# Five token chunks of a fused attention and feed-forward kernel, cut at other rows, with longer attention units

## The chip, the cores and the metric

The kernel runs on one core of a Trainium2 chip. The metric is the device time of one execution in microseconds (us). TensorE does the matmuls; VectorE, ScalarE and GpSimd (POOL) do element work; SyncE (SP) issues nearly all transfers.

## The reference

Four batches of eight heads, 576 positions, head dimension 64. Heads 0 to 3 attend to the last 32 positions (local), heads 4 to 7 to the positions of the same remainder by 32 (strided). The result, 2304 tokens by 512, goes through two feed-forwards:

```python
scores = np.where(masks[None, :, :, :], scale * np.matmul(q, k.transpose(0, 1, 3, 2)), -1000000000.0)
attn = np.exp(scores - np.max(scores, axis=-1, keepdims=True))
x = attn / (np.sum(attn, axis=-1, keepdims=True) + 1e-09) @ v
...
g = x @ w_gate
x = (g * (1.0 / (1.0 + np.exp(-g))) * (x @ w_val) @ w_out)
...
h = np.maximum(np.maximum(x @ w1, x @ w2), x @ w3)
out = h @ w_out
```

Sizes: w_gate and w_val 512 x 1536, w_out 1536 x 512; in the second, w1, w2, w3 512 x 768 and w_out 768 x 512.

## The kernel before

Work is counted in rows of 32 tokens: 72 rows, in the order ORDER. `ROWS` cuts that order into five chunks; `width(c)` is 32 times the rows of chunk c, at most 512 tokens.

**First feed-forward.** Its three weights lie in 12 blocks of 128 hidden units, counted by f. Every operand is split into a high and a low fp32r part, and a product is three matmuls (L701 high by high, L702, L703). For a chunk c and an f, `emit_gate` does 12 matmuls over the width of the chunk into a bank `ps_g`, and ScalarE's silu (L720) makes `ht`; `emit_val` does 12 into `ps_v`, and VectorE's L727 multiplies `ht` by it; ScalarE copies the high part (L733), GpSimd subtracts for the low part (L737); `emit_out` does 12 matmuls into four banks `ps_y`, one f later. That makes 36 matmuls for an f and 432 for a chunk. Gate and val banks come in turn from a pool of two, so val(f+1) reuses the bank that L727(f) reads.

**The x tiles.** `x_tile(c)` gives the high and low x of a chunk, with the tag `c % 2`: chunk c and chunk c+2 share memory. So writes into chunk 3's x wait until the last matmul that reads chunk 1's.

**Attention.** Chunk 0 and 1's attention comes ahead, in an order written out by hand. For c = 2 to 4, `attention_steps(c)` gives 15 lists of steps, and list i is emitted with slot (c-1) x 12 + i - 3, that is, during the chunk before. Local heads go in blocks of one or two groups of two rows: scores on TensorE (L393), minima against the mask on VectorE (L429), exponentials on ScalarE (L440), L445, L446 and L450 normalise on VectorE, then a transpose (L462), its copy (L467), the product with v (L504), and the copies into x, high by ScalarE (L516) and low by VectorE (L522). All of it goes through `att`, a pool of two banks. `scores_with` and `outputs_with` take two blocks at once; they call `claimed`, which asks for both banks and touches each by a tiny ScalarE copy (L309).

Strided rows that TensorE does not do go as `Unit`s of up to six rows on VectorE: products with the keys (L600) and their reductions (L603), one softmax for the unit (L608 to L615, with the exponential L610 on ScalarE), products with the values (L622) and reductions (L625), then transposes by threes (L632) into an `att` bank, and copies into x (L643 high, L644 low). The first matmuls of a gate read x's two blocks of local heads, the others the strided heads' blocks.

**Second weights.** `later` holds 60 steps that turn the second feed-forward's weights into the seven pieces of its scheme; each group of five steps is two loads, two conversions and a combination, then the parts (L281, L282) with their stores to `wsdr`. `PACE[c]` says how many steps are due in each f of chunk c (f below 10).

**The end.** From f = 10 of chunk 4 on the order is written by hand; in the slot before, the remaining w_v and w_o are reloaded, `load_y` (L838) loads the first tiles of y and `load_w` (L851) the second weights. The second feed-forward's matmuls are 128x384 (L858). Between, the scheduler places each engine's instructions.

Of the kernel before, what the change touches and what calls it, by code (L numbers as in the profile page):

```python
# [7 lines left out]
F32 = mybir.dt.float32  # L8
# [8 lines left out]
B, H, S, D = 4, 8, 576, 64  # L17
# [3 lines left out]
NI = S // STRIDE  # L21

LR = 2
# [8 lines left out]

PASSES = [1, 2, 0]

PACE = [0, 0.7, 1.4, 1.4, 3.1]

PACED = 10
NK = DM // 128

ROWS = [0, 16, 30, 44, 58, 72]  # L40


ORDER = [*range(16), *range(18, 72), 16, 17]
AT = {row: n for n, row in enumerate(ORDER)}
NC = len(ROWS) - 1
N = STRIDE * max(ROWS[c + 1] - ROWS[c] for c in range(NC))

ON_PE = [(0, 16, 4), (1, 14, 4)]

EARLY = -(-ROWS[1] // LR)  # L50

DEEP = [*range(NK // 2, NK), *range(NK // 2)]

# [40 lines left out]
def tile_attention_swiglu_maxout(  # L94
# [38 lines left out]
    tiny = sub(attn, "tiny", 2, side="right")  # L133
# [33 lines left out]

    ydr = [dram.tile([128, NK, width(c)], F32, name=f"ydr{c}") for c in range(NC)]

# [11 lines left out]
    st_p, pr_p = [], []  # L181
# [116 lines left out]
    def x_tile(c):  # L298
        if c not in xt:
            xt[c] = tuple(x_p.tile([128, NK, N], F32R, name=f"x{p}", tag=f"x{p}{c % 2}") for p in "hl")  # L300
        return xt[c]
# [222 lines left out]
    def local_block(g, home=None):  # L524


        def dst(src, us):
            for c, i0, i1, o in pieces(LR * g[0], LR * (g[-1] + 1)):
                t, w = slice(i0 * STRIDE, i1 * STRIDE), slice(o * STRIDE, (o + i1 - i0) * STRIDE)
                xh, xl = x_tile(c)  # L530
                yield xh[:, 0:2, t], xl[:, 0:2, t], src[:, :, w]

        return Block((locqk, locv), g[0], KB, [mask[0 if n % (NI // LR) == 0 else 1] for n in g], dst, home=home)
# [24 lines left out]
    def joined(ns):  # L558
        out = []
        for n in ns:  # L560
            if out and len(out[-1]) < 2 and out[-1][-1] + 1 == n:
                out[-1].append(n)
            else:
                out.append([n])
        return out

    class Unit:
# [36 lines left out]

        def softmax(self):
            sc, n, jn = self.sc, self.n, self.jn
            mx = tiny.tile([128, 6], F32, name="smx")[:, :n]
            nc.vector.tensor_reduce(mx, sc, AX.X, ALU.max)  # L608
            nc.vector.tensor_tensor(sc, sc, mx[:, :, None].to_broadcast([128, n, jn]), ALU.subtract)
            nc.scalar.activation(sc, sc, AF.Exp, scale=SCALE)  # L610
            sums = tiny.tile([128, 6], F32, name="ssum")[:, :n]
            nc.vector.tensor_reduce(sums, sc, AX.X, ALU.add)
            nc.vector.tensor_scalar(sums, sums, 1.0e-9, None, ALU.add)
            nc.vector.reciprocal(sums, sums)
            nc.vector.tensor_tensor(sc, sc, sums[:, :, None].to_broadcast([128, n, jn]), ALU.mult)  # L615
            self.o = st_p[0].tile([128, 6, D], F32, name="sto")

        def pv(self, r, eng):
            i = self.i0 + r
# [25 lines left out]

    def attention_blocks(c):
        rows = ORDER[ROWS[c]:ROWS[c + 1]]
        blocks = [local_block(g) for g in joined([r // LR for r in rows[::LR]])]
        if c == 1:
            blocks += [strided_block((st1qk, st1v), 1, g) for g in pairs(range(STRIDE // ON_PE[1][2]))]  # L650
        return blocks

    def attention_steps(c):

        steps = [[] for _ in range(15)]
        rows = ORDER[ROWS[c]:ROWS[c + 1]]
        eng = nc.vector
        blocks = attention_blocks(c)
        at = [0, 0, 4, 4, 8]
        for n, blk in enumerate(blocks):  # L660
            s0 = at[n]
            wait = 3 if c == 2 and s0 == 0 else 0
            steps[max(0, s0 - 2)].append(blk.load)
            if n % 2 and s0 == at[n - 1]:
                steps[s0].append(lambda a=blocks[n - 1], b=blk: a.scores_with(b))
                steps[s0 + wait].append(lambda a=blocks[n - 1], b=blk: (a.softmax(eng), b.softmax(eng)))
            elif n + 1 == len(blocks) or s0 != at[n + 1]:
                steps[s0].append(lambda blk=blk: (blk.scores(), blk.softmax(eng)))
            steps[s0 + (4 if wait else 1)].append(lambda blk=blk: blk.transpose(nc.scalar))
            if n % 2 and s0 == at[n - 1]:  # L670
                steps[s0 + (5 if wait else 2)].append(lambda a=blocks[n - 1], b=blk: (a.outputs_with(b), a.split(), b.split()))
            elif n + 1 == len(blocks) or s0 != at[n + 1]:
                steps[s0 + 2].append(blk.pv)
        units = []
        on_pe = {n: rows for n, rows, _ in ON_PE}
        left = [r for r in rows if r % NI >= on_pe.get(r // NI, 0)]
        while left:
            i = left[0]
            n = 1
            while n < len(left) and left[n] == i + n and (i + n) % NI % 6:  # L680
                n += 1
            units.append(Unit(i // NI, i % NI, n))
            left = left[n:]
        s0 = 0
        for u in units:
            steps[s0].append(u.load)
            steps[s0].append(u.begin)
            for r in range(u.n):
                steps[s0 + (2 * r // u.n)].append(lambda u=u, r=r: u.qk(r, eng))
            steps[s0 + 2].append(u.softmax)  # L690
            for r in range(u.n):
                steps[s0 + 2 + (2 * r // u.n)].append(lambda u=u, r=r: u.pv(r, eng))
            for r in range(0, u.n, 3):
                steps[s0 + 5 + r // 3].append(lambda u=u, r=r: u.out(r))
            s0 += 4
        return steps


# [5 lines left out]

    def linear(ps, w, x, n, ks=range(NK)):
        xh, xl = x
# [60 lines left out]
    def emit_out(c, f):  # L767
# [3 lines left out]
        if f == 0:  # L771
            yacc[c] = [acc.tile([128, 512], F32, name="ps_y", tag="acc") for _ in range(NK)]
        for m in range(NK):
            ms = slice(m * 128, (m + 1) * 128)
# [246 lines left out]
    if True:  # L1021
        blocks = [strided_block((st0,), 0, g, True) for g in pairs(range(STRIDE // ON_PE[0][2]))]
# [3 lines left out]
        def evictor(i):  # L1026
            return nc.vector if i in (0, 2, 3, 5, 6, 7) else nc.scalar

        steps = {
            "k": lambda i: nc.sync.dma_start(cst[:, halves[i]], shape_consts[:, halves[i]]),  # L1030
            "l": lambda i: blocks[i].load_qk(),
            "m": lambda i: blocks[i].load_v(),
            "S": lambda i: blocks[i].scores(),
            "W": lambda i: blocks[i].scores_beside(blocks[i + 1]),
            "M": lambda i: blocks[i].least(),
            "E": lambda i: blocks[i].exps(),
            "R": lambda i: blocks[i].inverse(),
# [42 lines left out]
        for s, (c, f) in enumerate(slots):  # L1080
# [7 lines left out]
            with ExitStack() as tied:  # L1088
                if c == 0:
                    tied.enter_context(tc.issue_after(last_val[0]))  # L1090
                for step in fill.get(s, []):
                    step()
            if c > 0 and f < PACED:
                due += PACE[c]
                with ExitStack() as tied:
# [25 lines left out]
    if True:  # L1121
# [13 lines left out]
        before = None  # L1135
        for p in range(NP):
            h2.clear()
            for g in range(NFP):
                for i in range(3):
# [12 lines left out]
                    before = grp  # L1152
            y = outputs(p, grp, y)
            before = None
# [99 lines left out]
```

## Time and profile before

| what | value |
| --- | --- |
| median of 3 runs | 785.83 us |
| lowest and highest | 784.95 and 786.53 us |
| the profiled execution | 786.19 us |
| its span, first to last instruction | 784.4 us |
| TensorE busy | 767.7 us |
| VectorE busy | 613.2 us |
| ScalarE busy | 400.9 us |
| GpSimd busy | 230.8 us |

The profile is of one execution. Starts count from the span's beginning. In it chunk 1's first gate begins at 140.54 us, chunk 2's at 237.47, chunk 3's at 334.42, chunk 4's at 428.47; the second feed-forward's steady part follows from 519.62 us. A matmul's duration in the profile overlaps the next one's, so its pace is read from start to start.

### The profile page before, as it was taken

To read this page: it belongs to the slowest core of one execution; us is meant where nothing else is said; L and a number is where in the kernel's file an instruction comes from. 1 tells how busy PE (TensorE), PEld (TensorE's weight loads), DVE (VectorE), ACT (ScalarE), POOL (GpSimd) and SP (SyncE) were. 2 spreads that over 40 slices of the span, in tenths; PEclk is the share of its full clock that TensorE was granted. 3 is DMA by queue.
4 is the path that set the end of the run, shared out by engine and by line. 5 is a ranking of instruction groups with operands and counts; after the bars stand their busy time and mean duration, and the time that the engine had idled before them with its cause. 6 is when DMAs were issued, how large, how long until landed. Compare 5 with 4: busy or idle time off the path is not lost.

```text
span 784.4 us, 13322 instructions
## 1 busy us (share of the span) xinstructions
PE 767.7 (98%) x4642; PEld 705.2 (90%) x4642; DVE 613.2 (78%) x1206; ACT 400.9 (51%) x925; POOL 230.8 (29%) x226
## 2 busy tenths in 40 slices
PE   5899999999999999999999999999999999999998
PEld 4677788888998998988899999999999999999998
DVE  5999999798959899799796777754689377855683
ACT  6999997644544636545342545432335233433342
POOL 2533332012221432325242556420124111321120
PEclk9999999999999999999999999999999999999999
DMA  9989886987657896847787999997675976878722
GB/s 274 369 277 320 306 351 236 372 252 230 221 188 222 285 293 222 267 168 256 255 286 267 314 378 392 342 377 274 242 276 199 414 270 264 276 280 355 276 101 81
DMA packets 75595, 216.26 MB, mean 276 GB/s; under 512 B 8488, under 2 KB 42024, under 8 KB 70920
## 3 DMA queue, kind: packets, MB, share of 16 engines
q1 hardware_dynamic: 75528, 215.41, 77.8%
q8 instruction: 37, 0.61, 0.3%
q14 instruction: 30, 0.25, 0.1%
HBM read 171.34 MB, written 44.04 MB: 275 GB/s over the span
## 4 chain that ended last, share of the span: by engine, by line
PE 85%; DVE 9%; ACT 3%; issue 1%; DMA 1%; POOL 1%; SPq 0%; DVEq 0%; ACTq 0%
PE ps_a L858 19%; PE ps_c L858 10%; PE ps_v L701 6%; PE ps_y L701 5%; PE ps_y L702 5%; PE ps_v L703 5%; PE ps_y L703 5%; PE ps_v L702 5%; PE ps_g L703 5%; PE ps_g L702 5%; PE ps_g L701 5%; PE ps_b L858 5%; DVE w L231 1%; PE ps_a L504 1%; PE ps_a L462 1%
## 5 line engine op out<-in xcount | busy, mean ns | idle before, releaser
L737 POOL TENSOR_TENSOR hl<-ht,hh 128x448 fp32r<-128x448 f32 x47 | 62.0, 1320 | 215.3 <-ACT hh L733 197.2
L869 ACT ACTIVATE s<-ps_a 128x384 f32<-128x384 f32 x99 | 48.5, 490 | 131.7 <-PE ps_a L858 131.7
L701 PE MATMUL ps_v<-xh,w_v 128*128 128x448 f32 (+1 forms) x240 | 90.8, 379 | 2.1 <-DVE ht L727 1.8
L701 PE MATMUL ps_g<-xh,wh_g 128*128 128x448 f32 (+1 forms) x240 | 89.9, 375 | 1.2 <-DVE ht L760 1.1
L702 PE MATMUL ps_y<-hl,w_o 128*128 128x448 f32 (+1 forms) x240 | 89.6, 373 | 0.0
L702 PE MATMUL ps_g<-xl,wh_g 128*128 128x448 f32 (+1 forms) x240 | 89.5, 373 | 0.0
L703 PE MATMUL ps_g<-xh,wl_g 128*128 128x448 f32 (+1 forms) x240 | 89.3, 372 | 0.0
L703 PE MATMUL ps_v<-xh,w_v 128*128 128x448 f32 (+1 forms) x240 | 89.2, 372 | 0.1
L703 PE MATMUL ps_y<-hh,w_o 128*128 128x448 f32 (+1 forms) x240 | 89.2, 372 | 0.0
L702 PE MATMUL ps_v<-xl,w_v 128*128 128x448 f32 (+1 forms) x240 | 88.9, 370 | 0.0
L733 ACT ACTIVATE hh<-ht 128x448 fp32r<-128x448 f32 (+1 forms) x60 | 35.3, 588 | 94.8 <-DVE ht L727 85.4
L701 PE MATMUL ps_y<-hh,w_o 128*128 128x448 f32 (+1 forms) x240 | 83.6, 376 | 0.0
L808 POOL TENSOR_TENSOR rT<-t,rT 128x384 f32<-128x384 f32 x9 | 12.5, 1392 | 147.1 <-DVE rT L807 147.1
L858 PE MATMUL ps_a<-y0hT,wr 128*128 128x384 f32 x162 | 54.1, 334 | 0.0
L858 PE MATMUL ps_a<-y1hT,wr 128*128 128x384 f32 x162 | 54.1, 334 | 0.0
L701 PEld LDWEIGHTS ps_v<-xh,w_v 128*128 128x128 f32 x240 | 45.1, 188 | 8.1 <-DVE ht L727 2.4
L701 PEld LDWEIGHTS ps_g<-xh,wh_g 128*128 128x128 f32 x240 | 45.1, 188 | 6.8 <-DVE ht L760 1.5
L703 PEld LDWEIGHTS ps_v<-xh,w_v 128*128 128x128 f32 x240 | 45.1, 188 | 5.5 <-DVE w_v L251 0.5
L701 PEld LDWEIGHTS ps_y<-hh,w_o 128*128 128x128 f32 x240 | 45.1, 188 | 5.2
L702 PEld LDWEIGHTS ps_g<-xl,wh_g 128*128 128x128 f32 x240 | 45.1, 188 | 5.1 <-DVE xl L522 0.3
L703 PEld LDWEIGHTS ps_g<-xh,wl_g 128*128 128x128 f32 x240 | 45.1, 188 | 5.1
L703 PEld LDWEIGHTS ps_y<-hh,w_o 128*128 128x128 f32 x240 | 45.1, 188 | 5.0 <-DVE w_o L251 0.3
(257 smaller groups left out, 2070.4 us busy)
## 6 DMA issues: line engine op xcount, KB each, us to landing
wr<-wsdr SPq DMA_DIRECT2D x36, 1792.0 KB, 8.1
raw<-in_w_dram SPq DMA_DIRECT2D x60, 512.0 KB, 6.3
w_v<-wvdr SPq DMA_DIRECT2D x48, 512.0 KB, 4.5
w_o<-wodr SPq DMA_DIRECT2D x48, 512.0 KB, 5.1
wsdr<-whi SPq DMA_DIRECT2D x36, 256.0 KB, 3.4
wvdr<-w_v SPq DMA_DIRECT2D x12, 512.0 KB, 4.6
wodr<-w_o SPq DMA_DIRECT2D x12, 512.0 KB, 6.6
wsdr<-w SPq DMA_DIRECT2D x24, 256.0 KB, 3.9
```

Source lines behind the costliest of these rows:

```text
L231: nc.vector.tensor_tensor(w, w, q, ALU.add)
L462: nc.tensor.transpose(ps[:sm.shape[2], g * 128:(g + 1) * 128], sm[:, g], ident)
L504: ins = nc.tensor.matmul(ps[j * D:(j + 1) * D, at:at + nq], v, p, start=True, stop=True).ins
L701: nc.tensor.matmul(ps, wh, xh, start=first, stop=False)
L702: nc.tensor.matmul(ps, wh, xl, start=False, stop=False)
L703: nc.tensor.matmul(ps, wl, xh, start=False, stop=last)
L733: return nc.scalar.activation(hs[c, f][0], t, AF.Copy).ins
L737: return eng.tensor_tensor(hl, t, f32(hh), ALU.subtract).ins
L808: nc.gpsimd.tensor_tensor(b12, self.raw["B22"], b12, ALU.subtract)
L858: nc.tensor.matmul(ps, w[:, c, a, ks], b, start=first and n == q == 0, stop=last and n == len(wts) - 1 and q == 2, skip_group_check=True,)
L869: nc.scalar.activation(s, ps, AF.Copy)
```

## The change

The rows are cut at 45 and 60 in place of 44 and 58, so the chunks have 512, 448, 480, 480 and 384 tokens. Since row 46 begins in the middle of a local group's two rows, a group that straddles a cut is now done with the earlier chunk (`attention_blocks`). Units have up to eight rows: a run of n rows that belong together is cut into equal parts of at most eight (the old cut was at multiples of six), and a chunk's units are spread over the 12 slots by their number, not four slots each. Eight units result where nine were. `PACE` is 2.0 in chunks 3 and 4 and was 1.4 and 3.1.

```diff
--- before.py
+++ after.py
@@ -32,12 +32,14 @@
 
 PASSES = [1, 2, 0]
 
-PACE = [0, 0.7, 1.4, 1.4, 3.1]
+PACE = [0, 0.7, 1.4, 2.0, 2.0]
 
 PACED = 10
+
+UNIT = 8
 NK = DM // 128
 
-ROWS = [0, 16, 30, 44, 58, 72]
+ROWS = [0, 16, 30, 45, 60, 72]
 
 
 ORDER = [*range(16), *range(18, 72), 16, 17]
@@ -604,16 +606,16 @@
 
         def softmax(self):
             sc, n, jn = self.sc, self.n, self.jn
-            mx = tiny.tile([128, 6], F32, name="smx")[:, :n]
+            mx = tiny.tile([128, UNIT], F32, name="smx")[:, :n]
             nc.vector.tensor_reduce(mx, sc, AX.X, ALU.max)
             nc.vector.tensor_tensor(sc, sc, mx[:, :, None].to_broadcast([128, n, jn]), ALU.subtract)
             nc.scalar.activation(sc, sc, AF.Exp, scale=SCALE)
-            sums = tiny.tile([128, 6], F32, name="ssum")[:, :n]
+            sums = tiny.tile([128, UNIT], F32, name="ssum")[:, :n]
             nc.vector.tensor_reduce(sums, sc, AX.X, ALU.add)
             nc.vector.tensor_scalar(sums, sums, 1.0e-9, None, ALU.add)
             nc.vector.reciprocal(sums, sums)
             nc.vector.tensor_tensor(sc, sc, sums[:, :, None].to_broadcast([128, n, jn]), ALU.mult)
-            self.o = st_p[0].tile([128, 6, D], F32, name="sto")
+            self.o = st_p[0].tile([128, UNIT, D], F32, name="sto")
 
         def pv(self, r, eng):
             i = self.i0 + r
@@ -645,7 +647,8 @@
 
     def attention_blocks(c):
         rows = ORDER[ROWS[c]:ROWS[c + 1]]
-        blocks = [local_block(g) for g in joined([r // LR for r in rows[::LR]])]
+        before = {r // LR for r in ORDER[:ROWS[c]]}
+        blocks = [local_block(g) for g in joined([g for g in dict.fromkeys(r // LR for r in rows) if g not in before])]
         if c == 1:
             blocks += [strided_block((st1qk, st1v), 1, g) for g in pairs(range(STRIDE // ON_PE[1][2]))]
         return blocks
@@ -677,22 +680,25 @@
         while left:
             i = left[0]
             n = 1
-            while n < len(left) and left[n] == i + n and (i + n) % NI % 6:
+            while n < len(left) and left[n] == i + n and (i + n) % NI:
                 n += 1
-            units.append(Unit(i // NI, i % NI, n))
+            parts = -(-n // UNIT)
+            for p in range(parts):
+                a, b = n * p // parts, n * (p + 1) // parts
+                units.append(Unit(i // NI, i % NI + a, b - a))
             left = left[n:]
-        s0 = 0
-        for u in units:
+        span = 12 // len(units)
+        for u, s0 in zip(units, range(0, 12, span)):
+            half = span // 2
             steps[s0].append(u.load)
             steps[s0].append(u.begin)
             for r in range(u.n):
-                steps[s0 + (2 * r // u.n)].append(lambda u=u, r=r: u.qk(r, eng))
-            steps[s0 + 2].append(u.softmax)
+                steps[s0 + half * r // u.n].append(lambda u=u, r=r: u.qk(r, eng))
+            steps[s0 + half].append(u.softmax)
             for r in range(u.n):
-                steps[s0 + 2 + (2 * r // u.n)].append(lambda u=u, r=r: u.pv(r, eng))
+                steps[s0 + half + half * r // u.n].append(lambda u=u, r=r: u.pv(r, eng))
             for r in range(0, u.n, 3):
-                steps[s0 + 5 + r // 3].append(lambda u=u, r=r: u.out(r))
-            s0 += 4
+                steps[min(14, s0 + span + 1 + r // 3)].append(lambda u=u, r=r: u.out(r))
         return steps
```

What moves, first on ScalarE, around the seam of chunks 1 and 2. The names: `sm` holds a local block's probabilities, `loct` its transposed ones, `ps_a` is a bank of `att`, and `stsc` a unit's scores. Before, the exponentials of chunk 3's first pair of blocks stand in chunk 1, between its ninth and its tenth silu:

```order
L720 ACTIVATE ht<-ps_g 128x448
L440 ACT_TABLE_LOAD
L440 ACTIVATE sm,stat<-sm,stat 128x96 x8
L733 ACTIVATE hh<-ht 128x448
L610 ACTIVATE stsc<-stsc 128x24
L720 ACT_TABLE_LOAD
L720 ACTIVATE ht<-ps_g 128x448
L643 ACTIVATE xh<-ps_a 64x2x96 x2
L733 ACTIVATE hh<-ht 128x448
```

With the change (line numbers are higher by two to six: L442 is L440, L469 is L467, L518 is L516, L645 is L643, L726 is L720, L311 is L309):

```order
L726 ACTIVATE ht<-ps_g 128x448
L518 ACTIVATE xh<-ps_a 128x2x32
L739 ACTIVATE hh<-ht 128x448
L311 ACTIVATE ps_a<-mh 1x1
L612 ACT_TABLE_LOAD
L612 ACTIVATE stsc<-stsc 128x126
L442 ACTIVATE sm,stat<-sm,stat 128x96 x8
L645 ACTIVATE xh<-ps_a 64x2x96
L469 ACTIVATE loct<-ps_a 96x512
L645 ACTIVATE xh<-ps_a 64x2x96
L469 ACTIVATE loct<-ps_a 96x512
L645 ACTIVATE xh<-ps_a 64x2x96
```

The exponentials of chunk 3's first pair stand behind the copy of 128x2x32 into chunk 3's x, and ahead of the first silu of chunk 2 (128x480, four rows further on); that copy stands behind the last silu of chunk 1.

TensorE at the same place, where gate and val of f = 0 in chunk 2 begin. Before:

```order
L703 MATMUL ps_y<-hh,w_o_2822 128x448
L701 MATMUL ps_g<-xh,wh_g_433 128x448
L702 MATMUL ps_g<-xl,wh_g_433 128x448
L703 MATMUL ps_g<-xh,wl_g_434 128x448
L701 MATMUL ps_g<-xh,wh_g_433 128x448
L702 MATMUL ps_g<-xl,wh_g_433 128x448
L703 MATMUL ps_g<-xh,wl_g_434 128x448
L701 MATMUL ps_v<-xh,w_v_2992 128x448
L702 MATMUL ps_v<-xl,w_v_2992 128x448
```

With the change (L395 is L393, L464 is L462, L634 is L632, L707 to L709 are L701 to L703):

```order
L709 MATMUL ps_y<-hh,w_o_2926 128x448
L708 MATMUL ps_y<-hl,w_o_2926 128x448
L709 MATMUL ps_y<-hh,w_o_2926 128x448
L634 MATMUL ps_a<-cst,sto 64x128 x3
L464 MATMUL ps_a<-cst,sm 96x128 x8
L634 MATMUL ps_a<-cst,sto 64x128 x3
L707 MATMUL ps_g<-xh,wh_g_433 128x480
L707 MATMUL ps_v<-xh,w_v_3017 128x480
L708 MATMUL ps_g<-xl,wh_g_433 128x480
```

Before, gate and val went on without attention work in between. Now the second half of their blocks stands behind three transposes of a unit, eight of the local pair, and three more of a unit; the pair's scores (L395) are a few rows higher, behind the first four of these `ps_y` matmuls.

SyncE, at the end of chunk 4, where the y tiles for the second feed-forward are loaded. Before:

```order
L284 DMA wsdr_147<-s_5611 128x2x256
L284 DMA wsdr_147<-whi 128x256
L284 DMA wsdr_147<-s_5612 128x256
L1018 DMA w_o_5753<-wodr_134 128x1024
L838 DMA y1lB_5777<-ydr_110 128x64
L838 DMA y1lB_5780<-ydr_108 128x256
L838 DMA y1lB_5780<-ydr_109 128x128
L1018 DMA w_o_5757<-wodr_135 128x1024
L851 DMA wr<-wsdr_139 128x3584
```

With the change (L844 is L838, L286 is L284, L1024 is L1018, L857 is L851):

```order
L1024 DMA w_o_5750<-wodr_135 128x1024
L286 DMA wsdr_147<-whi 128x2x256 x2
L286 DMA wsdr_147<-w_5589 128x2x256
L286 DMA wsdr_147<-w_5646 128x2x256
L286 DMA wsdr_147<-whi 128x2x256
L286 DMA wsdr_147<-s_5653 128x2x256
L286 DMA wsdr_147<-whi 128x256
L286 DMA wsdr_147<-s_5654 128x256
L844 DMA y1lB_5770<-ydr_110 128x32
L844 DMA y1lB_5773<-ydr_108 128x256
L844 DMA y1lB_5773<-ydr_109 128x128
L857 DMA wr<-wsdr_139 128x3584
```

The last w_o (`wodr_135`) stood behind the last loads of `y1lB` and now stands ahead of the stores of `wsdr_147` and of the last three of those loads.

## Rows read from the trace of the kernel before

**Rows 1.** The page, its parts 1 and 4: busy time of TensorE; shares of the chain.

```profile
PE 767.7 (98%) x4642; PEld 705.2 (90%) x4642; DVE 613.2 (78%) x1206; ACT 400.9 (51%) x925; POOL 230.8 (29%) x226
PE 85%; DVE 9%; ACT 3%; issue 1%; DMA 1%; POOL 1%; SPq 0%; DVEq 0%; ACTq 0%
```

**Rows 2.** Waits of TensorE from 145 to 525 us: total, times, longest us.

```profile
PE ps_v L701 <- DVE ht L727: 1.8, 2, 1.4
PE ps_v L701 <- ACT ht L720: 0.3, 1, 0.3
```

**Rows 3.** Timeline of TensorE, chunk 4: start us, us, engine, line, operation.

```profile
457.66 0.36 PE L701 MATMUL ps_g<-xh,wh_g 128*128 128x448 f32 x1
464.95 0.36 PE L701 MATMUL ps_g<-xh,wh_g 128*128 128x448 f32 x1
```

**Rows 4.** The same timeline, two gates in chunk 2.

```profile
301.80 0.37 PE L701 MATMUL ps_g<-xh,wh_g 128*128 128x448 f32 x1
309.24 0.37 PE L701 MATMUL ps_g<-xh,wh_g 128*128 128x448 f32 x1
```

**Rows 5.** The same timeline: 512 columns in chunk 0, 384 in the second feed-forward.

```profile
131.29 0.39 PE L701 MATMUL ps_g<-xh,wh_g 128*128 128x512 f32 x1
133.78 0.39 PE L703 MATMUL ps_g<-xh,wl_g 128*128 128x512 f32 x1
530.02 0.33 PE L858 MATMUL ps_a<-y0hT,wr 128*128 128x384 f32 x1
541.46 0.33 PE L858 MATMUL ps_c<-y0hB,wr 128*128 128x384 f32 x1
```

**Rows 6.** Groups of VectorE by line and shape: count, busy us, mean ns.

```profile
L445 DVE TENSOR_SCALAR stat<-stat 128x4 f32<-128x4 f32 x16 | 4.6, 285 | 4.6 <-ACT sm L440 4.6
L446 DVE RECIPROCAL stat<-stat 128x4 f32<-128x4 f32 x16 | 2.8, 175 | 0.3
L450 DVE TENSOR_TENSOR sm<-sm,stat 128x384 f32<-128x384 f32 x12 | 7.4, 616 | 0.1
L644 DVE TENSOR_TENSOR xl<-ps_a,xh 64x192 fp32r<-64x192 f32 x24 | 8.3, 346 | 1.8 <-ACT xh L643 1.4
L625 DVE TENSOR_REDUCE sto<-pr 128x64 f32<-128x768 f32 x2 | 1.9, 942 | 0.0
L622 DVE TENSOR_TENSOR pr<-stv,stsc 128x896 f32<-128x896 f32 x2 | 3.1, 1564 | 0.0
L622 DVE TENSOR_TENSOR pr<-stv,stsc 128x960 f32<-128x960 f32 x3 | 3.7, 1241 | 0.0
```

**Rows 7.** Timeline of ScalarE: the first and the last of six exponentials.

```profile
350.09 0.38 ACT L440 ACTIVATE sm<-sm,stat 128x96 f32<-128x96 f32 x1
351.90 0.36 ACT L440 ACTIVATE sm<-sm,stat 128x96 f32<-128x96 f32 x1
```

**Rows 8.** Windows, all engines: length, busy us (count) by engine, clock, DMA.

```profile
265.00:289.00 24.00, 24.00 (x142) 21.88 (x141) 23.94 (x35) 9.49 (x20) 9.52 (x9) 1.00 0.94 300
428.00:450.00 22.00, 22.00 (x111) 20.38 (x110) 13.37 (x18) 10.27 (x21) 10.85 (x10) 1.00 0.93 326
```

**Rows 9.** Timeline of SyncE's queue at the end of chunk 4: start us, us.

```profile
496.11 0.38 SPq L284 DMA_DIRECT2D wsdr<-whi  x1
501.74 0.40 SPq L1018 DMA_DIRECT2D w_o<-wodr  x1
502.19 1.39 SPq L838 DMA_DIRECT2D y1lB<-ydr  x3
```

**Rows 10.** Transfers from 485 to 510 us: count, KB each, median us to landing.

```profile
y1lB<-ydr SPq DMA_DIRECT2D x2, 128.0 KB, 3.3
```

**Rows 11.** A window near the start; columns as in rows 8.

```profile
15.00:20.00 5.00, 2.48 (x55) 1.80 (x53) 4.84 (x29) 4.76 (x18) 2.26 (x3) 1.00 1.05 315
```

**Rows 12.** The page, part 2: TensorE's granted clock in 40 slices.

```profile
PEclk9999999999999999999999999999999999999999
```

## The prediction

> **What bounds the kernel now.** First the page's busy shares and the shares of its chain: TensorE works 98% of the span and holds 85% of the chain that ends last [rows 1]. So the time is TensorE's matmuls at their pace, plus the moments in which it waits. The waits of TensorE over the four chunks of 448 tokens come next: three in all, 1.8 us for VectorE's product L727 (two times, the longest 1.4 us) and 0.3 us for ScalarE's L720 [rows 2]. There is almost nothing to win in waits, and every new wait is paid in full.
>
> The pace is read as starts in TensorE's timeline. In chunk 4, from one gate to the next, 36 matmuls of 448 columns and nothing else take 464.95 - 457.66 = 7.29 us, 202.6 ns each [rows 3]; in another stretch of the same kind 309.24 - 301.80 = 7.44 us, 206.7 ns [rows 4]. Over three chunks I take 203.2 ns as a mean, near the low row, because most undisturbed stretches have it. A matmul of 512 columns takes 2.49 us / 11 = 226.4 ns, one of 384 takes 11.44 us / 66 = 173.3 ns [rows 5]. The granted clock is at its upper level, 2.4 GHz, in all slices [rows 12], so a column takes 0.417 ns; above that lie 13.1 ns (512), 13.3 ns (384), and 16 to 20 ns (448).
>
> **Term 1, the widths.** Each chunk has 12 x 36 = 432 matmuls. Those of chunks 2, 3 and 4 go from three times 448 columns to 480, 480 and 384; the columns are as many as before, the matmuls too. What can change is the part beside the columns. For 480 there is no row: with the 13.3 ns of 512 and 384 it would take 213.3 ns, with the 20 ns of the slow stretch of 448 it would take 220 ns. I take 215, nearer the low end, since the two neighbours on both sides and the quick state of 448 (16 ns, so 216) lie there. The sum: (2 x 215 + 173.3 - 3 x 203.2) x 432 = **-2.7 us**, with ends -4.2 and +1.6 us. The Trainium skill, page "TensorE: Matmul & The Clock Gate", section "Back-to-back issue gap", gives an isolated matmul 2.5 ns above its columns, whatever their number; by it this term would be 0, as an estimate, because the columns stay. The rows here disagree with it: 13 to 20 ns, and more of it for 448 than for its neighbours.
>
> **Term 2, the wait at the end of chunk 1.** This is what the row limits do beside the widths. With 45 in place of 44, local group 23 (rows 46 and 47) is half in chunk 2, half in chunk 3. Its second half is written to chunk 3's x tiles, which are chunk 1's memory, so the copy of 128x2x32 (L516) waits for chunk 1's last val matmul, and until then the block holds its bank of the two that `att` has. Chunk 3's first pair of blocks needs both banks (`claimed`), so its scores come only there, as the ScalarE and TensorE orders above show: the exponentials of the pair and eight transposes stand between chunk 1's last out product and the third row block of chunk 2's first gate, with the last rows of a unit of six behind them. Before, nothing of the kind stood at this place.
>
> The chain behind the last score matmul, by rows of before: eight exponentials at (351.90 - 350.09) / 5 = 0.36 us [rows 7], the first some 0.4 us behind the scores for its minimum: 3.3 us. Then on VectorE L445, L446, a subtraction L644 and L450, 0.29 + 0.18 + 0.35 + 0.62 = 1.4; L644 again, 0.35; two reductions L625 that produce the unit's next rows, 0.94 and, with more elements, about 1.0; L644, 0.35; then, ahead of the fourth L644 in VectorE's order, two products L622 of 896 and 960 elements, 1.56 + 1.24 = 2.8; and that L644, 0.35 [rows 6]. Together 10.5 us, some 0.3 more with the hand-overs between engines. TensorE has in that time eight matmuls of 448 (1.65 us), 14 transposes at about 0.11 us (1.5), and two of 480 (0.4): 3.6 us. It waits for the rest, **+7.2 us**. Ends: 5.0, if VectorE does the reductions and products before the exponentials are done; 9.0, if the hand-overs cost as much as the 0.36 us between exponentials at each of some five steps. That it is 0 is excluded: TensorE's order is fixed, and it has no other work ahead of those transposes.
>
> Queued behind it on VectorE are two reductions and two products more, one further reduction, and the first L727 of chunk 2, about 7 us; TensorE has 25 matmuls of 480 and 16 small ones, 5.8 us, until val(2,1) needs that L727: **+1.3 us** (0 to 3).
>
> **Term 3, VectorE in chunks 1 and 2.** L727(f) must be done before val(f+1) starts; that is five products of 12 matmuls after val(f)'s end less one's own, 60 x 215 = 12.9 us in chunk 2. The eight rows of unit (3,0) and the new cut put into one such gap, ahead of L727 of chunk 2's f = 7, eight reductions L625, six products L622, five of L600 and L603, eight minima and two L644: by their sizes 12.8 to 14.5 us, then L727's own 0.6. It is late by 0.5 to 2.2 us; the next gap, 8.3 us of VectorE against 7.7 of TensorE, adds 0.5. I take **+2.0 us** (0 to 3.5). Against that the waits of before in chunks 2 and 3, 1.4 and 0.3 us [rows 2], go, because their places have less in front of them: **-1.7 us** (0 at worst). In chunk 1 one more gap is near full: **+0.5 us** (0 to 2). The other pace of the second weights moves six steps of VectorE work from chunk 4 into chunk 3. VectorE was busy 23.94 of 24 us from 265 to 289 us, but 13.37 of 22 from 428 to 450 [rows 8]; chunk 3 gets some 10 us of weight work (six steps at about 1.7) and loses some 4 of attention. I put it at nothing: 432 matmuls 12 ns longer give VectorE 5 us more. Without that cover it would be 1 to 2 us.
>
> **Term 4, the end of chunk 4.** In SP's order the last three y1lB loads now stand behind w_o of f = 11 and the eight wsdr stores; before, that w_o came after them. w_o's buffer is free once out(8) ends, one period of 36 x 173.3 ns = 6.2 us behind the start of gate(4,9), which I call T. The stores take 501.74 - 496.11 = 5.6 us, w_o 0.4, the loads 1.4 [rows 9], the landing 3.3 [rows 10]: T + 17, and the split of it about 1 more. TensorE wants it behind val(4,11), at T + 2 x 6.2 + 24 x 0.173 = T + 16.6. I take **+1.5 us** (0 to 3.5). The units' longer form itself, eight softmaxes for nine, is put at nothing: it takes short steps away and adds none beside those named.
>
> **Sum**: -2.7 + 7.2 + 1.3 + 2.0 - 1.7 + 0.5 + 1.5 = +8.1 us on the profiled run's 786.19 us (784.4 span and 1.8 around it) is 794.3; that run lies 0.36 above the median of the three, so 793.9, given as **794.0 us**.
>
> **The rivals.** *Faster*: the matmul of 480 has the overhead of 512 and 384 (-4.2 us), the old waits go (-1.7), and the wait at the boundary is under 3 us because VectorE and ScalarE run ahead. 786.2 - 5.9 + 2 = 782 to 784 us. For it speaks that 448 is the odd one among the widths [rows 3, 4, 5]; against it that 3.3 us of exponentials alone exceed what TensorE has there before its first transposes, 1.65 us. It decides at a new wait of 5.9 us. Chance 0.05. *No change*: the wait is 4 to 7 us and terms 3 and 4 stay hidden, as L727 was nearly everywhere before [rows 2]: 785 to 787.4 us; 0.09.
>
> *480 as dear as 512*, 226.4 ns: term 1 becomes (2 x 226.4 + 173.3 - 609.6) x 432 = +7.1 us, the time 804. For it: two widths of 448 and 512 show no even step. Against it: 384 and 512 do, to 0.2 ns. 0.06.
>
> *The clock falls* in the broken stretch at the boundary. TensorE worked 2.48 of the 5 us from 15 to 20 us and the granted clock stayed at 1.00, the upper level [rows 11]; the new gap is alike, but alone among full stretches. Were it at 1.2 GHz for the 10.5 us, its 3.6 us of work would take twice as long, and some of what follows: 798 to 801 us; 0.08. The Trainium skill, page "TensorE: Matmul & The Clock Gate", section "HAM oscillation — how this bites in real kernels", warns that waits between short bursts make the clock fall; the trace here so far does not bear it out, by the row just named.
>
> **How the numbers follow.** My forecast 0.72, the rivals 0.05, 0.09, 0.06 and 0.08. A change under 0.2% (1.6 us) can't be told from none here: faster 0.05, same 0.09, slower 0.86. The range is 787.0 to 800.5: below lie the faster case and most of the unchanged one, above the dear 480, together under 0.2. Within the forecast term 2's ends give 792 to 796, terms 3 and 4 at their ends 790 to 799.
>
> **What would show it.** Right: TensorE's waits name L644 or L643 and L450 at the seam of chunks 1 and 2, some 7 us, and L727 in chunk 2 near f = 8; a gate-to-gate period in chunks 2 and 3 of 7.74 us with nothing between; a short wait before the first L858. Wrong: no wait over 3 us at the seam, or a period of 7.65 us and less with L727 on time everywhere, or a granted clock below 1.00.

## The result and the profile after

The changed kernel takes 797.7 us (median of four, 796.96 to 798.0), the kernel before 785.9: ratio 1.015, 95% interval 1.0132 to 1.0167. It is slower, by 11.8 us. The profiled execution took 797.91 us with a span of 795.8, so the span grew by 11.4 us. The page's busy line and chain, which answer to [rows 1]:

```profile
PE 770.7 (97%) x4642; PEld 699.3 (88%) x4642; DVE 611.6 (77%) x1203; ACT 395.6 (50%) x923; POOL 233.0 (29%) x225
PE 74%; DVE 15%; ACT 4%; issue 3%; DMA 2%; POOL 1%; SPq 0%; DVEq 0%; ACTq 0%; POOLq 0%
```

TensorE has 3 us more of work on record and 11.4 us more of time: most of the growth is waiting. TensorE's waits from 130 to 540 us, without two of 0.3 and 0.2 us (columns as in [rows 2]; before there were three, 2.1 us together):

```profile
PE ps_g L707 <- ACT xh L645: 2.6, 1, 2.6
PE ps_v L707 <- DVE ht L733: 1.6, 3, 1.0
PE ps_a L464 <- ACT sm L442: 1.6, 1, 1.6
PE ps_a L864 <- DVE y1lB L180: 1.3, 1, 1.3
PE ps_a L464 <- DVE sm L452: 0.9, 1, 0.9
PE ps_g L708 <- DVE xl L646: 0.9, 1, 0.9
PE ps_y L707 <- ACT hh L739: 0.9, 1, 0.9
PE ps_b L864 <- ACT ysb L789: 0.9, 1, 0.9
```

Two places hold most of it. The first is the seam of chunks 1 and 2, in TensorE's timeline (start, duration, and in brackets the wait before):

```profile
241.53 0.49 PE L634 MATMUL ps_a<-cst,sto 128*64 128x128 f32 x3
243.58 0.61 PE L464 MATMUL ps_a<-cst,sm 128*96 128x128 f32 x4 [1.56 <-ACT sm L442]
245.12 0.62 PE L464 MATMUL ps_a<-cst,sm 128*96 128x128 f32 x4 [0.93 <-DVE sm L452]
245.61 0.52 PE L634 MATMUL ps_a<-cst,sto 128*64 128x128 f32 x3
248.71 0.77 PE L707 MATMUL ps_g<-xh,wh_g 128*128 128x480 f32 x1 [2.58 <-ACT xh L645]
250.80 0.77 PE L708 MATMUL ps_g<-xl,wh_g 128*128 128x480 f32 x1 [0.93 <-DVE xl L646]
251.37 0.60 PE L709 MATMUL ps_g<-xh,wl_g 128*128 128x480 f32 x1
251.77 0.60 PE L707 MATMUL ps_g<-xh,wh_g 128*128 128x480 f32 x1
...
255.64 0.49 PE L707 MATMUL ps_g<-xh,wh_g 128*128 128x480 f32 x1
```

Three transposes of a unit, a wait of 1.56 us for the exponentials, four of the local pair, 0.93 for the normalising, four more, and three of a unit; then 2.58 us for L645's copies and 0.93 for L646 before the gate's second half runs. From 241.53 to 250.80 us lie 9.3 us, with work for some 2. Behind that the matmuls of 480 columns come 0.40 us apart (251.37 to 251.77), because the granted clock is down to 1.2 GHz (windows; the clock is the number behind POOL):

```profile
247.00:248.00 1.00, 0.00 (x0) 0.00 (x0) 1.00 (x3) 0.00 (x0) 0.00 (x0) 0.50 0.00 0
252.00:253.00 1.00, 1.00 (x4) 0.79 (x4) 1.00 (x2) 0.00 (x0) 0.00 (x0) 0.50 0.00 0
254.00:255.00 1.00, 1.00 (x17) 0.64 (x17) 1.00 (x2) 0.99 (x2) 0.00 (x0) 1.00 0.00 0
```

The second place is the end of chunk 4. The chain of waits there, in order of time:

```profile
522.00 0.45 SPq L844
522.50 2.26 DMA y1lB<-ydr
...
526.21 0.54 DVE y1lB L180
526.75 0.47 DVE ht L733
527.25 0.03 ACT hh L739
```

A y1lB load issued at 522.0 us lands at 524.8. TensorE goes on at 526.34, with the first of its low parts; the last L733, which VectorE does after these, starts at 526.75, and its copy at 527.25. TensorE waits 1.3 us for y1lB, 0.9 for the copy L739, and 0.9 for an eviction L789. Ahead of the load SyncE's queue had stood still from 514.4 to 518.0 us, for a part of the second weights that VectorE makes. That is the longest of its waits from 498 to 524 us:

```profile
SPq L286 <- DVE w L284: 3.6, 1, 3.6
```

The paces, from starts in TensorE's timeline further on (480 columns in chunk 3; 384 in chunk 4, from val to val, 36 matmuls):

```profile
403.42 0.38 PE L707 MATMUL ps_v<-xh,w_v 128*128 128x480 f32 x1
...
405.80 0.38 PE L709 MATMUL ps_v<-xh,w_v 128*128 128x480 f32 x1
...
457.25 0.33 PE L707 MATMUL ps_v<-xh,w_v 128*128 128x384 f32 x1
...
463.49 0.33 PE L707 MATMUL ps_v<-xh,w_v 128*128 128x384 f32 x1
```

2.38 us / 11 = 216.4 ns, and 6.24 us / 36 = 173.3 ns. A matmul of 480 columns lies 16 ns above its columns, like 448 [rows 3], not 13 like 512 and 384 [rows 5].

### The profile page after: what moved, and what is told of

It reads as the page before. It is cut to its first block, busy times and chain, and to the rows that moved or that the text cites. A ratio compares the mean times of both kernels' runs of the same rounds, so it can differ in the third digit from the quotient of the medians.

```text
span 795.8 us, 13328 instructions
## 1 busy us (share of the span) xinstructions
PE 770.7 (97%) x4642; PEld 699.3 (88%) x4642; DVE 611.6 (77%) x1203; ACT 395.6 (50%) x923; POOL 233.0 (29%) x225
## 4 chain that ended last, share of the span: by engine, by line
PE 74%; DVE 15%; ACT 4%; issue 3%; DMA 2%; POOL 1%; SPq 0%; DVEq 0%; ACTq 0%; POOLq 0%
PE ps_a L864 19%; PE ps_c L864 9%; PE ps_b L864 5%; PE ps_v L707 5%; PE ps_y L707 4%; PE ps_y L708 4%; PE ps_y L709 4%; PE ps_v L708 4%; PE ps_v L709 4%; PE ps_g L707 4%; PE ps_g L708 4%; PE ps_g L709 4%; DVE pr L624 2%; DVE sto L627 2%; DVE stsc L605 1%
## 5 line engine op out<-in xcount | busy, mean ns | idle before, releaser
L743 POOL TENSOR_TENSOR hl<-ht,hh 128x480 fp32r<-128x480 f32 (+2 forms) x47 | 61.3, 1305 | 216.3 <-ACT hh L739 197.4
L707 PE MATMUL ps_g<-xh,wh_g 128*128 128x480 f32 (+3 forms) x240 | 90.5, 377 | 4.1 <-ACT xh L645 2.6
L707 PE MATMUL ps_v<-xh,w_v 128*128 128x480 f32 (+3 forms) x240 | 91.0, 379 | 1.9 <-DVE ht L733 1.6
L708 PE MATMUL ps_g<-xl,wh_g 128*128 128x480 f32 (+3 forms) x240 | 89.8, 374 | 1.0 <-DVE xl L646 0.9
L709 PE MATMUL ps_g<-xh,wl_g 128*128 128x480 f32 (+3 forms) x240 | 89.5, 373 | 0.0
L708 PE MATMUL ps_y<-hl,w_o 128*128 128x480 f32 (+3 forms) x240 | 89.2, 372 | 0.0
L709 PE MATMUL ps_v<-xh,w_v 128*128 128x480 f32 (+3 forms) x240 | 89.0, 371 | 0.0
L708 PE MATMUL ps_v<-xl,w_v 128*128 128x480 f32 (+3 forms) x240 | 89.0, 371 | 0.0
L709 PE MATMUL ps_y<-hh,w_o 128*128 128x480 f32 (+3 forms) x240 | 88.8, 370 | 0.0
L739 ACT ACTIVATE hh<-ht 128x480 fp32r<-128x480 f32 (+3 forms) x60 | 35.2, 587 | 104.7 <-DVE ht L733 91.0
L707 PE MATMUL ps_y<-hh,w_o 128*128 128x480 f32 (+3 forms) x240 | 83.8, 374 | 0.9 <-ACT hh L739 0.9
L707 PEld LDWEIGHTS ps_g<-xh,wh_g 128*128 128x128 f32 x240 | 45.3, 189 | 11.3 <-ACT xh L645 2.8
L864 PE MATMUL ps_a<-y0hT,wr 128*128 128x384 f32 x162 | 54.1, 334 | 0.0
L864 PE MATMUL ps_a<-y1hT,wr 128*128 128x384 f32 x162 | 54.1, 334 | 0.0
L707 PEld LDWEIGHTS ps_v<-xh,w_v 128*128 128x128 f32 x240 | 45.3, 189 | 9.2 <-DVE ht L733 3.2
L733 DVE SCALAR_TENSOR_TENSOR ht<-ht,ps_v 128x480 f32<-128x480 f32 (+2 forms) x48 | 29.4, 613 | 30.9 <-PE ps_v L709 25.9
L707 PEld LDWEIGHTS ps_y<-hh,w_o 128*128 128x128 f32 x240 | 45.0, 188 | 6.6 <-ACT hh L739 1.2
L709 PEld LDWEIGHTS ps_v<-xh,w_v 128*128 128x128 f32 x240 | 45.2, 188 | 5.9 <-DVE w_v L253 0.5
L709 PEld LDWEIGHTS ps_g<-xh,wl_g 128*128 128x128 f32 x240 | 45.4, 189 | 5.4
```

Of the source, the lines that this page charges most:

```text
L707: nc.tensor.matmul(ps, wh, xh, start=first, stop=False)
L708: nc.tensor.matmul(ps, wh, xl, start=False, stop=False)
L709: nc.tensor.matmul(ps, wl, xh, start=False, stop=last)
L733: m = nc.vector.scalar_tensor_tensor(t, t, 1.0, ps[:, :n], ALU.mult, ALU.mult).ins
L739: return nc.scalar.activation(hs[c, f][0], t, AF.Copy).ins
L743: return eng.tensor_tensor(hl, t, f32(hh), ALU.subtract).ins
```

## The experiments

All ratios are to the kernel before, on the same chip. The first question is whether the seam is the cause, or one of the three parts by itself.

**1. The seam undone.** The cut at 45 falls between rows 46 and 47 (ORDER leaves 16 and 17 for the end), the two rows of local group 23. Here the group is computed with both chunks, and each keeps its own row:

```diff
             for c, i0, i1, o in pieces(LR * g[0], LR * (g[-1] + 1)):
+                if only is not None and c != only:
+                    continue
...
-        before = {r // LR for r in ORDER[:ROWS[c]]}
-        blocks = [local_block(g) for g in joined([g for g in dict.fromkeys(r // LR for r in rows) if g not in before])]
+        blocks = [local_block(g, only=c) for g in joined(list(dict.fromkeys(r // LR for r in rows)))]
```

> The changed kernel (797.7 us) with one part undone: the local group that the cut at 45 divides is computed twice, with each chunk for its own row, so nothing of chunk 2's blocks is written to chunk 3's x tiles; widths, units and pace stay. Theory (the bank held until chunk 1's last val product makes the wait at the seam of chunks 1 and 2, 7.3 us of it by the trace and 1.4 us for the clock that falls in it): 788 to 790 us, no wait of TensorE over 1.5 us between 225 and 260 us, granted clock 1.00 throughout. Rival (the longer units keep VectorE busy, and TensorE would wait there for it in any case): 795 us or more, with waits for L733 or L646 in place of those for L645.

793.59 us, ratio 1.011 (1.0093 to 1.0126). TensorE's waits from 200 to 262 us:

```profile
PE ps_v L708 <- DVE ht L734: 3.6, 3, 1.8
PE ps_g L708 <- ACT ht L727: 1.3, 1, 1.3
PE ps_g L709 <- DVE xl L648: 0.3, 1, 0.3
```

The wait for the transposes and for L645 is gone and the granted clock stays up from 225 to 260 us. But only 3 to 4 of the 11.8 us go, because 5.2 us of other waits stand in the same stretch, for L733 (L734 here) above all, one of them 1.8 us long where none over 1.5 was expected. Each theory held in part: the seam does what was said of it, and waits for VectorE, the rival's, are there too, behind it. The group done twice is itself work; how much of the 5.2 us that makes is not separated.

**2. Units of up to eight alone** (the kernel before, with `UNIT` and the new spread).

```diff
+UNIT = 8
...
+            parts = -(-n // UNIT)
+            for p in range(parts):
+                a, b = n * p // parts, n * (p + 1) // parts
+                units.append(Unit(i // NI, i % NI + a, b - a))
```

> The kernel before with the units of up to eight rows alone; old cuts of rows, old pace. Theory of the seam: 785 to 787.5 us, the units as such cost little, since both their products and their reductions are as many as before. Rival of the units: 790 us or more, with new waits of val products for L733 in chunks 1 to 3 of 3 us and more together.

790.59 us, 1.0079 (1.0066 to 1.0093): the rival's number. Its waits from 200 to 262 us, and VectorE's timeline there:

```profile
PE ps_v L707 <- DVE ht L733: 3.2, 3, 1.7
PE ps_g L707 <- ACT ht L726: 0.7, 1, 0.7
```

```profile
214.41 2.85 DVE L602 TENSOR_TENSOR pr<-stk,stq 128x768 f32<-128x768 f32 x2
217.18 1.87 DVE L605 TENSOR_REDUCE stsc<-pr 128x12 f32<-128x768 f32 x2
...
224.11 0.17 DVE L447 TENSOR_SCALAR stat<-stat 128x4 f32<-128x4 f32 x1 [1.57 <-ACT sm L442]
...
225.19 0.61 DVE L733 SCALAR_TENSOR_TENSOR ht<-ht,ps_v 128x448 f32<-128x448 f32 x1
...
227.65 2.85 DVE L602 TENSOR_TENSOR pr<-stk,stq 128x1024 f32<-128x1024 f32 x2
...
234.95 0.60 DVE L733 SCALAR_TENSOR_TENSOR ht<-ht,ps_v 128x448 f32<-128x448 f32 x1
```

Chunk 3's first unit now has the eight rows 10 to 17 of a batch, the longest there are; before, it had two of them. Their key products (L602, 704 to 1152 columns) and reductions (L605) take up most of VectorE's time in the last three f of chunk 1, and L733 comes at 225.19 and 234.95 us, some 6.5 us after the last product of its val; TensorE waits for it. Ahead of the first of the two VectorE also stood idle, 1.57 us for ScalarE's exponentials (L442), longer than TensorE's wait of 1.19 us there: the order has a part in it beside the work. The waits from 145 to 545 us are 3.2 us more than before; the rest of the 5.7 us is not placed.

**3. The pace alone.**

```diff
-PACE = [0, 0.7, 1.4, 1.4, 3.1]
+PACE = [0, 0.7, 1.4, 2.0, 2.0]
```

> The kernel before with the paces 2.0 and 2.0 of chunks 3 and 4 alone. Theory of the seam: 785 to 787.5 us, six steps of weight work moved from chunk 4 into chunk 3 are hidden. Rival (the last step, a slot later, and what is queued on SyncE behind it delay the first y tiles): 788 to 790 us, with a wait for y1lB of 1.3 us or more before the first L858, as in the changed kernel.

790.35 us, 1.0069 (1.0056 to 1.0082). The rival's size, but not its place: nothing waits at the end of chunk 4. TensorE's waits for VectorE from 350 to 450 us, the clock behind the longest, which lasts from 423.5 to 426.2, and all of chunk 3, from its first gate to chunk 4's, here and in the kernel before (windows; behind the length, VectorE's busy time is the third):

```profile
PE ps_v L701 <- DVE ht L727: 3.4, 2, 2.7
```

```profile
426.00:427.00 1.00, 0.77 (x2) 0.72 (x3) 1.00 (x3) 0.79 (x2) 0.13 (x1) 0.50 1.09 282
333.55:432.66 99.11, 95.39 (x532) 85.65 (x531) 93.80 (x141) 45.70 (x97) 42.42 (x34) 0.98 0.79 265
334.42:428.47 94.05, 93.76 (x533) 84.65 (x532) 84.14 (x130) 40.85 (x87) 31.16 (x27) 1.00 0.72 240
```

The 5 us lie in chunk 3: 99.1 us in place of 94.1. The six steps of weight work lie there on a VectorE that is nearly full, 93.8 of 99.1 us.

**4. The cuts at 46 and 60** in the changed kernel: no group is divided.

```diff
-ROWS = [0, 16, 30, 45, 60, 72]
+ROWS = [0, 16, 30, 46, 60, 72]
```

> The changed kernel with the second cut at 46 in place of 45, so no group is divided: chunks of 512, 448, 512, 448, 384 tokens. Theory of the seam: no wait at the seam, as in the first of these runs, and the widths are cheaper than 480 twice, (226.5 + 203.2 - 2 x 216.5) ns x 432 = -1.4 us: 786.5 to 788.5 us. Rival of the units: 794 us or more.

800.46 us, 1.0197 (1.0184 to 1.021). The theory of the seam fails here: with no divided group it is slower still, with nine waits for L733 (5.7 us) and 2.0 for L726 between 145 and 450 us.

**5. The old pace in the changed kernel** (`PACE` as before).

> The changed kernel with the old pace of the second weights (1.4 and 3.1). By itself the new pace cost 5 us, nearly all in one wait for L727 in chunk 3 (2.7 us) with the clock down behind it. Theory (that place has cover in the changed kernel: matmuls of 480 columns leave VectorE 13 ns more each, and TensorE waits nowhere in its chunk 3): 796.5 to 799 us, ratio 1.014 to 1.018. Rival (the pace costs its 5 us in the changed kernel too): 791 to 793 us, ratio 1.007 to 1.010.

800.55 us, 1.0195 (1.0167 to 1.0222). The rival falls: what costs 5 us by itself costs nothing here, and rather saves up to 3 (the two intervals meet at 1.0167). The traces agree: chunk 3 takes as long with either pace, though VectorE is busy for 10.7 us more with the new one. The same window, in the changed kernel and in this run:

```profile
349.98:448.43 98.45, 98.22 (x514) 83.89 (x513) 87.79 (x134) 46.20 (x96) 41.04 (x34) 1.00 0.79 269
351.10:449.60 98.50, 98.27 (x514) 83.87 (x513) 77.06 (x121) 40.64 (x84) 28.99 (x27) 1.00 0.70 237
```

With 1.4 and 3.1 there is a new wait of 1.0 us for a w_o and 0.7 for L726 in chunk 4; part of the difference is a longer dip of the clock at the seam (245 to 255 us), so no more than the sign is taken from it.

**6, 7, 8. The old kernel at other even cuts**: old units, old pace, no divided group; only `ROWS` is changed, to 46 and 60, 46 and 58, 42 and 58.

```diff
-ROWS = [0, 16, 30, 44, 58, 72]
+ROWS = [0, 16, 30, 46, 60, 72]
```

> The kernel before with cuts at 46 and 60 (512, 448, 512, 448, 384 tokens), no group divided, old units, old pace. Theory A (units and pace made the fourth run's 14 us, cuts cost only at the end): the widths give (226.5 + 203.2 + 174.5 - 609.8) ns x 432 = -2.4 us, the three waits at the end with 384 tokens in chunk 4 (y1lB, hh, ysb; 2.5 to 3.5 us in the changed kernel) cost about 2.5: 784 to 787 us. Theory B (each new cut moves attention work among the chunks, and VectorE is late wherever the sum comes out worse): 789 us or more, with waits for L727 of 4 us and more in all in chunks 1 to 3.

> The kernel before with cuts at 46 and 58 (512, 448, 512, 384, 448 tokens): the last chunk stays at 448. Theory A: -2.4 us for the widths, no waits at the end: 782.5 to 784.5 us, ratio 0.996 to 0.9995. Theory B: 787 us or more; waits for L727 in chunk 1, which has 16 strided rows to do in the time of 448 tokens, and in chunk 3, short at 384.

> The kernel before with cuts at 42 and 58 (512, 448, 384, 512, 448 tokens). Theory A: 782.5 to 784.5 us. Theory B: chunk 2 has 384 tokens, so VectorE has 40 x 12 x 30 ns = 13 us less time in it, for more attention (16 rows of chunk 3): 790 us or more, with the waits for L727 in chunk 2.

(In the last, the product is 36 x 12 x 30 ns.) 796.57, 797.76 and 797.74 us; 1.0133 (1.0106 to 1.0159), 1.0157 (1.013 to 1.0183), 1.0153 (1.0127 to 1.018). The times are theory B's in all three, and run 4's loss is for two thirds there without the new units and the new pace. The widths were as cheap as said (226.5 to 227.5 ns for 512, 174 to 176 for 384). Waits from 145 to 450 us came to 5.0, 8.7 and 9.0 us. In the third most of them sit in chunk 2, 235 to 330 us, but the engine named for the longest is another than expected:

```profile
PE ps_g L701 <- ACT ht L720: 4.7, 2, 2.8
```

Before, the waits there were 2.1 us, so they account for 3 to 7 us of the 10 to 12. Run 6 has the three waits at the end of chunk 4 too, 1.1 us for y1lB, 0.9 and 0.9; the granted clock is at 0.50 for some 3 us in runs 6 and 7 and some 10 us in run 8. The rest is not placed, so a late VectorE, theory B's cause, is shown for a part of the loss only.

**9 and 10. Chunk 3's units two slots later**, in run 1 and in run 2.

```diff
+            if c == 3:
+                s0, half = (2, 3) if s0 == 0 else (8, 2)
```

> The first of these runs (the divided group computed on both sides, 793.6 us) with chunk 3's first unit begun two slots later and its second two slots later too. That first unit has seven long rows, 14.7 us of key products and reductions, which lay in the last slots of chunk 1, whose waits for VectorE are 5.3 us there (169 to 257 us). Theory (the size of the unit that begins in chunk 1's last slots makes VectorE late there): those waits fall to 2 us or less, 788 to 790.5 us, ratio 1.004 to 1.007. Rival (every rearrangement of VectorE's work brings waits somewhere, the place alone changes): 792 us or more, with as much waiting in chunk 2.

> The kernel before with the units of up to eight alone (790.6 us), and chunk 3's units begun two slots later in the same way. Its waits for VectorE were 5.6 us, 4.4 of them between 220 and 236 us, in front of which stand the products of the unit of eight long rows. Theory: 785.5 to 787.5 us, ratio 1.001 to 1.003. Rival: 789 us or more.

795.17 us, 1.0121 (1.0107 to 1.0136), and 791.07, 1.0068 (1.0055 to 1.0081): as without it. But neither tested its theory. VectorE's timeline in the second has the same products at the same place as in run 2:

```profile
215.51 2.84 DVE L602 TENSOR_TENSOR pr<-stk,stq 128x768 f32<-128x768 f32 x2
218.28 1.86 DVE L605 TENSOR_REDUCE stsc<-pr 128x12 f32<-128x768 f32 x2
```

The slot in which a step is written doesn't hold it back: the scheduler draws the products forward into whatever time it sees on VectorE.

**11. The seam filled**: in the changed kernel, 12 products of a zero block, added into the gate's bank where TensorE waited longest.

```diff
+            if fill and k == 2:
+                with tc.issue_after(Unit.turned):
+                    for _ in range(fill):
+                        nc.tensor.matmul(ps, zeros, xh[:, 0, :n], start=False, stop=False)
```

> The changed kernel with 12 matmuls of a zero weight block added into chunk 2's first gate bank, in the long wait at the seam, between the unit's transposes and the gate's second half; the sums stay as they are. Theory (the clock fell since TensorE had little to do there, and that cost 1.4 us beside the waits): granted clock 1.00 from 240 to 260 us, the eight matmuls behind the wait 0.22 us apart in place of 0.40, 1.0 to 1.6 us less: 796.1 to 796.8 us, ratio 1.0125 to 1.0145. Rival (the clock's fall lies under VectorE's chain and costs nothing, since val(2,1) waits for VectorE's product anyway): 797.5 to 798.5 us.

796.35 us, 1.0137 (1.0117 to 1.0156): the expected number, but the interval reaches that of the changed kernel, so the time alone decides nothing. TensorE's timeline and the clock:

```profile
246.58 3.63 PE L719 MATMUL ps_g<-xh,zeros 128*128 128x480 f32 x12
...
251.60 0.49 PE L710 MATMUL ps_g<-xl,wh_g 128*128 128x480 f32 x1 [0.95 <-DVE xl L648]
...
255.05 0.48 PE L709 MATMUL ps_g<-xh,wh_g 128*128 128x480 f32 x1
```

```profile
246.00:247.00 1.00, 1.00 (x6) 0.89 (x5) 0.03 (x1) 0.63 (x2) 0.00 (x0) 0.50 0.00 0
250.00:251.00 1.00, 0.65 (x3) 0.21 (x2) 1.00 (x2) 0.00 (x0) 0.00 (x0) 1.00 0.00 0
```

The clock fell all the same, at 245 us, ahead of the filling, but was up again by 249 in place of 253.8. The same stretch, from the gate's second half to the next gate, took 255.05 - 251.60 = 3.45 us in place of 255.64 - 250.80 = 4.84: 1.4 us, as said. Half of that was lost ahead of it: counted from the first three transposes (241.63 us, before 241.53), the gate's second half began 10.0 us later in place of 9.3.

**12. A small unit first**: run 1 with chunk 3's units cut to 1, 6 and 8 rows.

```diff
+            cuts = [n * p // parts for p in range(parts)] + [n]
+            if c == 3 and i // NI == 2:
+                cuts = [0, 1, n]
```

> The first of these runs (divided group on both sides, 793.6 us, ratio 1.011) with chunk 3's units cut to 1, 6 and 8 rows in place of 7 and 8, so that a small unit comes first, as in the kernel before. A unit has one tile for its scores (stsc, one buffer), so the next unit's key products wait until the first unit's values are through, and the scheduler cannot draw seven long rows of them into the end of chunk 1, where it drew them whatever slot they were written in. Theory (that tile is the throttle, and the unit's size took it away): the waits between 200 and 260 us fall from 5.0 to 2 us or less, 788.5 to 791 us, ratio 1.004 to 1.007; what is left are the 2.5 us at the end of chunk 4. Rival (VectorE has too much to do there in any order): 793 us or more, ratio 1.010 or more, the waits a chunk later.

792.58 us, 1.0093 (1.007 to 1.0115): between the two. Waits from 200 to 262 us fall from 5.2 to 3.8 only, and 1.3 us appear in chunk 2 (here the waits from 200 to 350 us):

```profile
PE ps_v L710 <- DVE ht L736: 3.3, 2, 2.0
PE ps_g L710 <- ACT ht L729: 1.8, 2, 1.6
```

The key products did leave chunk 1's last f, yet VectorE is late a little further on. That the one tile of scores is the throttle isn't shown.

## Why the prediction was right, and where it wasn't

The time lay in the range, on the side that was forecast, 3.7 us above the number. The mechanism that carries the forecast, the wait at the seam, is there. That the sum is near is in part luck, since misses of both signs stand in it. By its own steps:

- **Term 1, the widths: said -2.7 us, measured about -0.7.** 480 columns take 216.4 ns in the stretch shown, and 216.6 as a mean over the undisturbed matmuls of chunks 2 and 3, not 215; those of 384 in chunk 4 have 174.7 as their mean, for 173.3 in the best stretch: (2 x 216.6 + 174.7 - 609.6) x 432 = -0.7. The step that failed is the choice of the low end for its neighbours in width; the quick state of 448 [rows 3] was the right row.
- **Term 2, the seam: said +7.2, measured 9.3 - 2.0 = 7.3** (the 2.0 are 14 transposes at 0.11 us and two products). The chain of named instructions from the pair's scores to the fourth L646 was 10.5 to 10.8 us, and was 250.8 - 239.7 = 11.1. What stood behind it went otherwise. val(2,1) didn't wait for L733 (+1.3 said): VectorE was done with it 6.2 us behind the fourth L646 and not 7 (256.95 us), and TensorE, slow itself, reached val(2,1) only at 258.36. The clock fell, which I had as a rival at 0.08 and as a sign of being wrong, and cost 1.4 us in run 11's comparison, not the 4 to 7 of that rival. That waits between short stretches of matmuls bring the clock down is the rule of the Trainium skill, page "TensorE: Matmul & The Clock Gate", section "HAM oscillation — how this bites in real kernels". The rows of the seam agree with it, with 0.50 at 247 us; those of [rows 11], where it stayed at 1.00, do not.
- **Term 3, VectorE: said +2.0 - 1.7 + 0.5 = +0.8, measured 0.** The wait near f = 8 of chunk 2 wasn't there; outside the seam and the end, waits are 2.1 us after and 2.1 before, half of the former at a place that no term named, 1.04 us for L733 in f = 3 of chunk 2 (276.4 us). Two sizes failed. TensorE's gap was not 12.9 us: from val(6)'s last product to val(8) were 319.83 - 305.25 = 14.6, because TensorE also had the attention's own matmuls in it. And VectorE's work in that gap, put at 12.8 to 14.5 us, took 11.1 (306.30 to 317.38 us), so L733, done at 318.0, would have been in time for the 12.9 as well. What I didn't weigh at all is the unit of long rows at the end of chunk 1: in the changed kernel 0.2 us of waits stand there, ahead of the seam, but runs 1 and 2 show it as waits of 4 to 5 us.
- **Pace: said 0, "hidden by the longer matmuls of 480".** Runs 3 and 5 bear out that it is hidden, not its price: without cover +5.4 us (I said 1 to 2), with it none. Nor are the longer matmuls all of the cover: by the windows of runs 3 and 5 chunk 3 is 4.4 us longer than before, and VectorE has 7.1 us less of other work in it (77.1 us busy in place of 84.1, both at the old pace; I said some 4). Which of the two is needed is not separated.
- **Term 4, the end: said +1.5, measured +3.0.** The wait for y1lB, 1.3 us, has about the size said, but by two errors that cancel. With T = 505.1 us, y1lB lands at T + 19.7 and not T + 17, because the stores ahead of it wait 3.6 us for VectorE's L284; w_o itself was issued when said, at 511.6. And TensorE wants y1lB at T + 19.9 and not T + 16.6, because twelve products of out and three L858 (L864 here) come before. The new order on SyncE isn't needed for the wait: run 6 has the old one, with the last w_o behind these loads, and still waits 1.1 us; run 3 has w_o ahead of the stores and 448 tokens in chunk 4, and no wait. A wait for y1lB stands only in runs whose chunk 4 has 384 tokens, in all of them but run 12. The two waits behind it, for L739 and L789, were not in the sum.

The sum by measured terms: -0.7 + 7.3 + 1.4 + 0 + 3.0 = 11.0 of the span's 11.4 us. Up to chunk 1's first gate, where both kernels do the same, the changed one was 0.8 us quicker in these two executions (139.73 us for 140.54), so behind that 1.2 us are not placed.

The terms describe the changed kernel, but they don't say what each part of the change is worth by itself. Units alone cost 6 us, the pace alone 5, new cuts alone 10 to 12, together some 22; the change as a whole costs 11.8. (The cuts at 45 and 60 were not run alone; the 10 to 12 are of others.) Undoing the seam gave back 3 to 4, not the 8.7 of its wait and its clock. My reading, which no run isolates, is that VectorE has one slack to spend in each f, and whoever comes second finds it spent. Whether some other arrangement makes use of wide and narrow chunks is open; the four tried here don't, and no version that was run beats the kernel before.

## What to carry to other kernels

Where TensorE is busy 98% of the span and another engine works nearly as long between its hand-overs, an order that fits can be worth more than cheaper shapes: here three sets of cheaper widths, worth 2.4 us, each came out 10 to 12 us slower. A cost that is hidden should be written down with the thing that hides it, since a change in one part takes the cover from another: read it from each engine's order over the whole stretch, and measure parts both alone and taken away. An edit that only writes steps later doesn't move them where a scheduler places the work; check in the trace where the work went.

## What was not expected of the hardware

The clock. In the changed kernel it fell to 1.2 GHz at 247 us, within the seam's wait of 2.58 us and after two others of 1.56 and 0.93, and stayed there to 253.8 us, for matmuls 0.40 us apart in place of 0.22. In run 3 it fell in a wait of 2.7 us begun at 423.5. In runs 4, 6, 8 and 12 it fell in or just behind waits of 1.9 to 2.8 us, in run 7 behind two of 0.8 and 0.9; yet a wait of 2.0 us up to 380 us in run 4 left it at 1.00. In the kernel before, TensorE works half of the time from 15 to 20 us [rows 11] and the clock stays up; in runs 1, 3 and 4, whose work up to there is the same, it was at 1.2 GHz for 3 to 7 us between 19 and 28 us. So one trace in which it didn't fall is no proof that it won't.

A matmul's time above its columns isn't even in the width: in the quickest stretches read it is 13 ns at 384 and 512 columns, 16 at 448 and 480.
